# Windowed attention and a snake-activated MLP on one Trainium2 core: where the global rows are turned, cast and placed

## The chip, the core and the metric

The kernel runs on one core of a Trainium2 chip. The metric is the device time of one execution in microseconds (us). The core has five engines with an instruction queue each: TensorE (PE, its weight loads PEld), VectorE (DVE), ScalarE (ACT), GpSimd (POOL) and SyncE (SP). SP computes nothing; it issues DMAs. POOL issues DMAs too, and casts while it loads. Each queue runs in the order in which the program wrote it.

## What is computed

For each of 8 batches there are 8 heads of 576 rows of 64 numbers. A row attends to the rows at most 32 away; 8 rows are global: they see all and are seen by all. The result, 4608 tokens of 512 numbers, goes through two matrix products with a snake activation between them.

```python
def _attn_ref(q, k, v, global_idx):
    scores = scale * np.matmul(q, k.transpose(0, 1, 3, 2))
    mask = np.abs(pos[:, None] - pos[None, :]) <= 32
    mask = mask | is_global[:, None] | is_global[None, :]
    scores = np.where(mask, scores, -1e9)
    attn = softmax(scores)
    return np.matmul(attn, v)

def _moe_ref(x, w_in, w_out, alpha):      # x 4608x512, w_in 512x2048, w_out 2048x512
    h = x @ w_in
    s = np.sin(alpha * h)
    return (h + s * s / (alpha + 1e-09)) @ w_out
```

## The kernel before, in words

The order of all work is written out by hand; waits follow from the tiles that an instruction reads and writes.

**Stages.** After a setup comes attention(0) alone. Then, for b = 0 to 7, gemm1(b) (the product with w_in and the activation), and attention(b+1), with the matmuls of gemm2(b) (the product with w_out) put in between. gemm2(b) is a generator; `fill(n)` issues its next n matmuls (128x512 each) on TensorE. LATE gives these numbers for attention(1) by head pair and third of scores, MIDST those after the last pair, GROUP_LATE those for gemm1(1) by product, 64 in all. What is not used up goes on later.

**Attention of a batch** goes over four head pairs (hp). For each, `scores` makes three groups of four matmuls into a PSUM ring of two (line 737), ScalarE takes the exponential (line 745), VectorE multiplies it by MASK (line 748). The products of the pair before (line 779) stand between: with VX (values) into zn, with OB (ones) into zd. Then `inverse` (lines 805 and 808, ScalarE), `sums` (line 789) and `normalise` (line 811, VectorE) make xT. `beside(hp)` ends a pair: what the caller wants done there. `idle(hp)` issues a 128x512 matmul of ones (`warm`, line 537) whose result nobody reads.

**Tiles of keys, queries and values.** KX, QX and VX exist twice; batch b uses number b % 2. Batch 0's keys and queries are loaded by rows and turned on TensorE (`turn_part`, `place_part`, lines 584 to 605). Batch b > 0: `cast_qk(b)` (POOL, line 328) casts q and k in DRAM to kd and qd, `turn_qk(b)` (SP, line 337) turns them by two DMA transposes into kt and qt, and `place` (VectorE, lines 347 and 354) copies those into KX and QX, in PLACES: four copies of keys, then four of queries. `load_v(b)` (POOL, line 385) loads values, four DMAs for each pair.

**Global rows.** `gather(src, dst)` (SP, line 480) issues eight DMAs that fetch the global rows of all batches: gk, gq and gv. They lie in the rows 13, 14 and 15 of H2 that gemm1 fills later with its products 13 to 15 (gq in 13, gk in 14, gv in 15). `turn_kq` turns gk and gq in eight TensorE transposes (line 701) and casts them on VectorE to kTg and qTg (line 705); `place_globals(b)` (POOL, lines 363 and 368) copies those into KX and QX. `cast_globals_v` (POOL, line 693) casts gv to VGb, from which `load_vg(b)` (SP, line 394) brings eight pieces to VX.

**gemm1(b)** makes 16 products (nt) of eight matmuls (line 967) in three PSUM tiles in turn; each goes through a sine on ScalarE (line 1003), a square on ScalarE if nt is in ON_ACT and otherwise on VectorE (lines 1008 and 1010), and a last step on VectorE (line 1014). In gemm1(0), at nt = 10, POOL has a tiny copy `seen` that waits for kt, and then issues V of batch 1, place_globals(1), w_out (`load_w_out`, line 408) and more V. At nt = 10 to 13 the first two pairs of batch 1's keys and queries are placed; the other two pairs are placed in attention(1), in beside(0) and beside(1).

Before the change the setup queues gk, batch 0's load_vg, gq and gv on SP one after the other; beside(0) of attention(0) places the second half of batch 0, clears VX[1] and QX[1] on POOL, queues cast_globals_v on POOL and the two transposes of batch 1 on SP; beside(1) calls turn_kq; KX[1] is cleared by VectorE in four parts, one in the setup and three in beside(0) to beside(2).

Of the kernel before, what the change touches and what calls it, by code (L numbers as in the profile page):

```python
# [28 lines left out]
PLACES = [(w, t, y) for w in (1, 0) for t in range(2) for y in range(2)]  # L29
# [218 lines left out]
def kernel(  # L248
# [93 lines left out]
    def place(b, which, t, y, copy, hps=slice(0, NHP)):  # L342
# [10 lines left out]
        else:  # L353
# [2 lines left out]
                in_=src.rearrange("p h (i a) -> p h i a", a=24),  # L356
            )

    def place_globals(b):

        for t in range(2):
            rows = slice(t * D, (t + 1) * D)
            nc.gpsimd.tensor_copy(
                out=KX[b % 2][rows, :, :, t * D + KT : t * D + KT + NG],
                in_=kTg[rows, :, None, :, b].to_broadcast([D, NHP, NT12, NG]),
            )
        for y in range(2):
            nc.gpsimd.tensor_copy(
                out=globals_of(b, slice(0, P), y),
                in_=qTg[:, :, None, y::2, b].to_broadcast([P, NHP, 7, 4]),  # L370
            )
# [106 lines left out]
    def gather(src, dst):  # L478
        for j in range(NG):
            nc.sync.dma_start(  # L480
                out=dst[j * B : (j + 1) * B],
                in_=src[:, :, bass.ds(greg[j], 1), :].rearrange("b h o d -> b h (o d)"),
            )
# [73 lines left out]
    load_w_in((2, 3))  # L557
    load_vg(0)
    gather(q, gq)
    gather(v, gv)  # L560


    band = setup.tile([P, 2, 2, WCOL // 2], DT.bfloat16, name="band")
# [69 lines left out]

    gpf = setup.tile([P, 1], DT.float32, name="gpf")
    nc.vector.tensor_copy(out=gpf[:], in_=gp64[:].bitcast(DT.int32)[:, 0:1])
    place_part(1, 0, 0, act)
    nc.scalar.activation(out=qpos[:], in_=qpos[:], func=AF.Square, bias=gpf[:, 0:1], scale=-1.0)
    place_part(1, 0, 1, act)
    gf = setup.tile([P, NG], DT.float32, name="gf")
    nc.vector.tensor_copy(out=gf[:], in_=gidx8[:].bitcast(DT.int32)[:, 0::2])  # L640
    first = setup.tile([P, NG], DT.float32, name="first")
# [12 lines left out]
    )  # L654
    nc.vector.tensor_tensor(out=fone[:], in0=fone[:], in1=cond[:, 2:3], op=ALU.mult)

    nc.vector.memset(KX[1][:, 0], 0.0)
    for n in range(2):
        place_part(0, 0, n, dve)
    for w, name in ((1, "k"), (0, "q")):  # L660
        pg[w] = both[0:D, 32 + w * 64 : 64 + w * 64].bitcast(DT.bfloat16)
        nc.tensor.transpose(
# [29 lines left out]
    def cast_globals_v():  # L692
        nc.gpsimd.tensor_copy(out=VGb[:], in_=gv.rearrange("p h d -> p (h d)"))
# [19 lines left out]
    def attention(b, beside):  # L713
# [101 lines left out]

        start, per_scores = (START, PER_SCORES) if b != 1 else (0, LATE)
        def idle(hp):
            if (b == 0 and hp > 1) or (b == 1 and hp < 3):
                warm(zo[0], 1)

        fill(start)
# [1 line left out]
        for hp in range(NHP):  # L823
            Es[hp] = pairp.tile([P, NT12, WCOL], DT.bfloat16, name="E")
            for g in range(2):
                scores(hp, g)
                fill(per_scores[hp][g])
                idle(hp)
            if b == 0 and hp:
                products(hp - 1, range(3), (1,))  # L830
            elif hp:
                products(hp - 1, (0, 1))
            scores(hp, 2)
            idle(hp)
            if b == 0 and hp:
                products(hp - 1, range(3), (0,))
            elif hp:
                products(hp - 1, (2,))
            if hp:
                inverse(hp - 1)  # L840
                sums(hp - 1, 1)
                sums(hp - 1, 0)
                normalise(hp - 1)
            fill(per_scores[hp][2])
            beside(hp)
# [96 lines left out]


    ON_ACT = (1, 3, 5, 8, 10, 12, 14)
    ON_ACT_FIRST = (1, 3, 4, 6, 7, 9, 10, 11, 12, 13, 14)
    ON_ACT_SECOND = (1, 3, 4, 5, 9, 10, 11, 12, 13, 14)

    def gemm1(b):


        xT = xTs[b]
        r0 = (b % 2) * S
        NE = NG * B // 2
        more = b == B - 1
        W = HALF + (NE if more else 0)
        xg = XG[:].rearrange("p c j b -> p c (j b)")
        hr = tc.alloc_tile_pool(name="hr", bufs=1, space=PSUM)
        hs = {}

        def chunks(nt, cs):  # L960
            if nt not in hs:
                hs[nt] = (zn, None, zd)[nt % 3] or hr.tile([P, 2, 512], DT.float32, name="zr")
            h = hs[nt]
            for c in cs:
                for e in range(2):
                    lhsT = w_in[:, c, nt * P : (nt + 1) * P]
                    nc.tensor.matmul(  # L967
                        out=h[:, e, 0:HALF], lhsT=lhsT, rhs=xT[:, c, e, :],
                        start=(c == 0), stop=(c == CT - 1), skip_group_check=True,
                    )  # L970
                    if more:
                        nc.tensor.matmul(
                            out=h[:, e, HALF:W], lhsT=lhsT, rhs=xg[:, c, e * NE : (e + 1) * NE],
                            start=False, stop=(c == CT - 1), skip_group_check=True,
                        )

        on_act = (ON_ACT_FIRST, ON_ACT_SECOND, ON_ACT)[min(b, 2)]
        for nt in range(NT):
            if b < 2 and 10 <= nt < 14:
                for which, t, y in PLACES[2 * (nt - 10) : 2 * (nt - 9)]:  # L980
                    place(b + 1, which, t, y, nc.vector.tensor_copy, slice(0, NHP if b else 2))
            if b == 1 and nt in (3, 4):
                square_x(0, nt - 3)
            if b == 1 and nt in (6, 8):
                square_w(nt // 2 - 3)
            if b == 0 and nt == 10:

                nc.gpsimd.tensor_copy(out=seen[:], in_=turned[1][1][0:1, 0:1])
                load_v(1, (0,))
                place_globals(1)  # L990
                load_v(1, (1,))
                load_w_out()
                load_v(1, (2, 3))
                load_vg(1)
            if nt == 0:

                for n in range(2):
                    chunks(n, range(CT - 1))
            chunks(nt, range(CT - 1, CT) if nt < 2 else range(CT))
            h = hs[nt]  # L1000
            fill((GROUP_LATE if b == 1 else PER_GROUP)[nt])
            sb = spool.tile([P, 2, HALF + NE], DT.bfloat16, name="sb")
            nc.scalar.activation(  # L1003
                out=sb[:, :, 0:W], in_=h[:, :, 0:W], func=AF.Sin, scale=alphaT[:, nt : nt + 1]
            )
            s2 = spool.tile([P, 2, HALF + NE], DT.bfloat16, name="s2")
            if nt in on_act:
                nc.scalar.activation(out=s2[:, :, 0:W], in_=sb[:, :, 0:W], func=AF.Square)  # L1008
            else:
                nc.vector.tensor_tensor(out=s2[:, :, 0:W], in0=sb[:, :, 0:W], in1=sb[:, :, 0:W], op=ALU.mult)  # L1010
            for dst, lo, hi in (
                (H2[:, nt, r0 : r0 + S], 0, HALF), (HG[:, nt, :], HALF, HALF + NE)
            )[: 1 + more]:
                nc.vector.scalar_tensor_tensor(  # L1014
                    out=dst.rearrange("p (e c) -> p e c", e=2),
                    in0=s2[:, :, lo:hi], scalar=recipT[:, nt : nt + 1], in1=h[:, :, lo:hi],
                    op0=ALU.mult, op1=ALU.add,
                )
        hr.release()
# [50 lines left out]
    START = 2  # L1070
    PER_SCORES = ((1, 11, 3), (3, 3, 4), (3, 3, 4), (3, 4, 5))

    LATE = ((0, 0, 0), (0, 0, 0), (0, 0, 0), (4, 4, 6))
    MIDST = 4
    PER_GROUP = (0, 0, 5) + 11 * (1,) + (0, 0)
    GROUP_LATE = (0, 0, 4) + 10 * (3,) + (4, 4, 4)

    def places_at(b_att, at):
        if b_att == 1 or b_att + 1 == B:
# [5 lines left out]
    def phase_a(b_att, b_moe):  # L1085
        def beside(at):

            if b_moe is None:
                if at == 0:
                    second_half()  # L1090
                    nc.gpsimd.memset(VX[1][:].bitcast(DT.int32), 0)
                    nc.gpsimd.memset(QX[1][:].bitcast(DT.int32), 0)
                    cast_globals_v()
                    turn_qk(1)
                if at == 1:
                    turn_kq()
                if 0 <= at < 3:
                    nc.vector.memset(KX[1][:, at + 1], 0.0)
                return
            if at == 0:  # L1100
                if b_moe == 2:
                    column_norms(zn[:, 0, :])
                if b_moe >= 3:
                    token_norms(b_moe - 3, zn[:, 1, :])
            if 0 <= at < 2 and b_moe:
                square_x(b_moe, at)
            if b_att == 1 and 0 <= at < 2:
                for which, t, y in PLACES[4 * at : 4 * at + 4]:
                    place(1, which, t, y, nc.vector.tensor_copy, slice(2, NHP))
            for which, t, y in places_at(b_att, at):  # L1110
                place(b_att + 1, which, t, y, nc.vector.tensor_copy)
            if b_moe == 0 and at == 2:
                turn_qk(2)
            if b_moe == 1 and at in (2, 3):
                square_w(at)

        if b_moe is not None:
            waiting.append(gemm2(b_moe))
        attention(b_att, beside)
# [67 lines left out]
```

## Time and profile before

| what | value |
|---|---|
| median of 3 runs | 400.41 us (400.18 to 401.48) |
| the profiled execution | 398.71 us, of which the span is 396.9 us |
| granted TensorE clock in it | 0.999 |
| TensorE busy | 343.0 us, 86% of the span |
| ScalarE, VectorE, GpSimd busy | 294.8, 289.5, 129.7 us |
| DMA moved | 38.08 MB, mean 96 GB/s |

A profile is of one execution. Its span runs from the first to the last instruction; the execution's own time also holds what lies around it. A line such as "zo L701 <- DMA H" names the tile that is written, the line of the kernel and, behind the arrow, what ended the wait; buffer numbers are left out, so that gk, gq and gv all appear as H. A wait is put down to one releaser, which need not be the right one where several DMAs write the same tile.

### The profile page before, as it was taken

How to read it: one execution, taken by the hardware profiler on the slowest of the kernel's cores; microseconds unless marked ns; L12 is line 12 of the kernel's file. 1: busy time of each engine (PE TensorE's matmuls, PEld its weight loads, DVE VectorE, ACT ScalarE, POOL GpSimd, SP SyncE). 2: the span in 40 equal slices, each digit the busy share in tenths (PEclk: the TensorE clock that was granted, in tenths of full speed). 3: DMA queues.
4: the chain of work that ended last, by engine and by line, in shares of the span. 5: the costliest groups of instructions: out<-in, count | busy, mean ns of one | idle time of the engine just before them, and what ended most of it. 6: DMA issues, size and time to landing. Idle time of an engine off the chain costs nothing. (4 is left out here: it accounts for less than half of the span.)

```text
span 396.9 us, 8633 instructions
## 1 busy us (share of the span) xinstructions
PE 343.0 (86%) x3175; PEld 233.6 (59%) x3175; DVE 289.5 (73%) x614; ACT 294.8 (74%) x564; POOL 129.7 (33%) x203
## 2 busy tenths in 40 slices
PE   2621888589999889999999999999999999899893
PEld 2511756366666556667666776667667766576341
DVE  6940778857786988897889888888887876588500
ACT  7740699868987978878887888798888888776111
POOL 8890674677204730085008500870000000000001
PEclk9999999999999999999999999999999999999999
DMA  7999899999975794568907991562610001001221
GB/s 119 118 172 158 145 122 175 174 163 136 157 135 87 85 141 90 90 85 95 210 28 86 104 201 55 58 64 43 136 28 28 26 28 55 20 8 28 55 81 46
DMA packets 103579, 38.08 MB, mean 96 GB/s; under 512 B 94138, under 2 KB 98250, under 8 KB 103082
## 3 DMA queue, kind: packets, MB, share of 16 engines
q0 software_dynamic: 56640, 18.56, 40.8%
q1 hardware_dynamic: 46890, 18.89, 22.6%
q8 instruction: 27, 0.44, 0.5%
q14 instruction: 22, 0.18, 0.2%
HBM read 37.15 MB, written 17.83 MB: 139 GB/s over the span
## 5 line engine op out<-in xcount | busy, mean ns | idle before, releaser
L1027 PE MATMUL zo<-w_out,H 128*128 128x512 bf16 x576 | 152.7, 378 | 0.0
L967 PEld LDWEIGHTS <-w_in 128*128 128x128 bf16 x1024 | 99.3, 97 | 47.4 <-issue 16.1
L385 POOL DMA_DIRECT2D VX<-in_v_dram x128 | 83.7, 667 | 121.1 <-PE zd L779 103.3
L745 ACT ACTIVATE E<-ring 128x480 bf16<-128x480 f32 x96 | 54.3, 569 | 41.9 <-PE ring L737 41.3
L1027 PEld LDWEIGHTS <-H 128*128 128x128 bf16 x576 | 52.1, 97 | 38.0
L967 PE MATMUL zn<-xT,w_in 128*128 128x288 bf16 x384 | 57.3, 285 | 4.1 <-DVE H L1014 3.8
L748 DVE TENSOR_TENSOR E<-E,MASK 128x480 bf16<-128x480 bf16 x96 | 38.2, 428 | 17.7 <-ACT E L745 16.3
L967 PE MATMUL zr<-xT,w_in 128*128 128x288 bf16 x320 | 47.9, 285 | 1.2 <-DVE H L1014 0.7
L967 PE MATMUL zd<-xT,w_in 128*128 128x288 bf16 x320 | 46.6, 285 | 0.9 <-DVE H L1014 0.7
L1014 DVE SCALAR_TENSOR_TENSOR H<-s,recipT,zn 128x576 bf16<-128x576 bf16 x48 | 39.0, 813 | 9.2 <-ACT s L1008 5.9
L737 PE MATMUL ring<-QX,KX 128*128 128x120 bf16 x384 | 37.7, 223 | 9.3 <-ACT E L745 4.3
L1008 ACT ACTIVATE s<-sb 128x576 bf16<-128x576 bf16 (+1 forms) x63 | 43.4, 689 | 2.0
L1003 ACT ACTIVATE sb<-zn,alphaT 128x576 bf16<-128x576 f32 (+1 forms) x48 | 35.6, 741 | 12.2 <-PE zn L967 8.8
L737 PEld LDWEIGHTS <-KX 128*128 128x128 bf16 x384 | 28.4, 101 | 24.2 <-issue 9.7
L1055 POOL DMA_INDIRECT out_dram<-osb,grow x1 | 1.0, 1004 | 125.6 <-SPq L1155 125.6
L1014 DVE SCALAR_TENSOR_TENSOR H<-s,recipT,zd 128x576 bf16<-128x576 bf16 x40 | 32.6, 814 | 7.3 <-ACT s L1008 5.3
L1010 DVE TENSOR_TENSOR s<-sb 128x576 bf16<-128x576 bf16 (+1 forms) x65 | 30.1, 464 | 8.4 <-ACT sb L1003 8.2
L1014 DVE SCALAR_TENSOR_TENSOR H<-s,recipT,zr 128x576 bf16<-128x576 bf16 x40 | 32.5, 813 | 5.1 <-ACT s L1008 3.0
L1033 ACT COPY osb<-zo 128x512 f32<-128x512 f32 x36 | 20.8, 578 | 20.4 <-PE zo L1027 20.4
L1003 ACT ACTIVATE sb<-zd,alphaT 128x576 bf16<-128x576 f32 (+1 forms) x40 | 29.7, 741 | 6.9 <-PE zd L967 3.8
L779 PEld LDWEIGHTS <-VX 128*128 128x128 bf16 x448 | 26.5, 100 | 12.2 <-issue 6.8
L1003 ACT ACTIVATE sb<-zr,alphaT 128x576 bf16<-128x576 f32 (+1 forms) x40 | 29.6, 739 | 4.4 <-PE zr L967 3.3
(158 smaller groups left out, 448.5 us busy)
## 6 DMA issues: line engine op xcount, KB each, us to landing
VX<-in_v_dram POOLq DMA_DIRECT2D x128, 36.0 KB, 2.7
kd<-in_k_dram POOLq DMA_DIRECT2D x7, 576.0 KB, 6.1
qd<-in_q_dram POOLq DMA_DIRECT2D x7, 576.0 KB, 9.0
w_in<-in_moe_w_in_dram POOLq DMA_DIRECT2D x4, 512.0 KB, 8.9
w_out<-in_moe_w_out_dram POOLq DMA_DIRECT2D x4, 512.0 KB, 10.0
out_dram<-osb SPq DMA_DIRECT2D x8, 256.0 KB
out_dram<-osb SPq DMA_DIRECT2D x8, 224.0 KB
out_dram<-osb SPq DMA_DIRECT2D x8, 192.0 KB
```

What stands on the lines that cost most here:

```text
L385: nc.gpsimd.dma_start(out=VX[b % 2][r : r + 24, hp, :, t * D : t * D + D], in_=v[b, 2 * hp + t].rearrange("(i a y) d -> y a i d", a=24, y= ...
L737: nc.tensor.matmul(out=ps[:, e * WCOL : (e + 1) * WCOL], lhsT=kx[:, hp, i, :], rhs=qx[:, hp, :, s0 : s0 + 60], start=True, stop=True, skip ...
L745: nc.scalar.activation(out=Eg, in_=ps[:, 0 : 4 * WCOL], func=AF.Exp, scale=scale, accum_out=EA[:, n : n + 1])
L748: nc.vector.tensor_tensor(out=Eg, in0=Eg, in1=MASK[:, 4 * g : 4 * g + 4, :].rearrange("p i c -> p (i c)"), op=ALU.mult,)
L779: nc.tensor.matmul(out=out_t[:, half, :, a - half * CUT : z - half * CUT], lhsT=OB[:] if key else VXb[:, hp, i, :], rhs=E[:, i, :, a - s0 ...
L967: nc.tensor.matmul(out=h[:, e, 0:HALF], lhsT=lhsT, rhs=xT[:, c, e, :], start=(c == 0), stop=(c == CT - 1), skip_group_check=True,)
L1003: nc.scalar.activation(out=sb[:, :, 0:W], in_=h[:, :, 0:W], func=AF.Sin, scale=alphaT[:, nt : nt + 1])
L1008: nc.scalar.activation(out=s2[:, :, 0:W], in_=sb[:, :, 0:W], func=AF.Square)
L1010: nc.vector.tensor_tensor(out=s2[:, :, 0:W], in0=sb[:, :, 0:W], in1=sb[:, :, 0:W], op=ALU.mult)
L1014: nc.vector.scalar_tensor_tensor(out=dst.rearrange("p (e c) -> p e c", e=2), in0=s2[:, :, lo:hi], scalar=recipT[:, nt : nt + 1], in1=h[:, ...
L1027: nc.tensor.matmul(out=ops[:], lhsT=H2[:, nt, blk * P : (blk + 1) * P], rhs=w_out[:, nt, :], start=(nt == 0), stop=(nt == NT - 1),)
L1033: nc.scalar.copy(out=osb[:], in_=ops[:])
```

## The change

- v's global rows are gathered behind the two transposes of batch 1 in SP's queue, in beside(0), and no longer in the setup.
- turn_kq moves from beside(1) of attention(0) into gemm1(0), ahead of product 9. cast_globals_v moves from beside(0) into gemm1(0), at nt = 10, behind the first four V loads and ahead of place_globals(1).
- In the setup the placing of the first half of batch 0's queries (VectorE) comes ahead of the small mask operations, and both halves of the keys (ScalarE) ahead of a square. KX[1] is cleared in four parts in beside(0) to beside(3).
- In attention(1) the keys of the last two pairs are still placed in beside(0); their queries are placed in pair 1 ahead of inverse, sums and normalise of pair 0, and no longer in beside(1).
- The matmuls of ones in pair 2 of attention(1) go; eight matmuls of gemm2(0) take their place (LATE), taken from gemm1(1) (GROUP_LATE).
- In gemm1(0) the squares of products 4 and 6 go to VectorE, that of 5 to ScalarE.

```diff
+    def place_rest(which):
+        for w, t, y in PLACES:
+            if w == which:
+                place(1, w, t, y, nc.vector.tensor_copy, slice(2, NHP))
...
     gather(q, gq)
-    gather(v, gv)
...
-    place_part(1, 0, 0, act)
+    for n in range(2):
+        place_part(1, 0, n, act)
     nc.scalar.activation(out=qpos[:], in_=qpos[:], func=AF.Square, bias=gpf[:, 0:1], scale=-1.0)
-    place_part(1, 0, 1, act)
+    for n in range(2):
+        place_part(0, 0, n, dve)
...
-    nc.vector.memset(KX[1][:, 0], 0.0)
-    for n in range(2):
-        place_part(0, 0, n, dve)
...
-            if (b == 0 and hp > 1) or (b == 1 and hp < 3):
+            if (b == 0 and hp > 1) or (b == 1 and hp < 2):
                 warm(zo[0], 1)
...
+            if b == 1 and hp == 1:
+                place_rest(0)
             if hp:
                 inverse(hp - 1)
...
-    ON_ACT_FIRST = (1, 3, 4, 6, 7, 9, 10, 11, 12, 13, 14)
+    ON_ACT_FIRST = (1, 3, 5, 7, 9, 10, 11, 12, 13, 14)
...
+            if b == 0 and nt == 9:
+                turn_kq()
             if b == 0 and nt == 10:
                 nc.gpsimd.tensor_copy(out=seen[:], in_=turned[1][1][0:1, 0:1])
                 load_v(1, (0,))
+                cast_globals_v()
                 place_globals(1)
...
-    LATE = ((0, 0, 0), (0, 0, 0), (0, 0, 0), (4, 4, 6))
+    LATE = ((0, 0, 0), (0, 0, 0), (2, 3, 3), (4, 4, 6))
-    GROUP_LATE = (0, 0, 4) + 10 * (3,) + (4, 4, 4)
+    GROUP_LATE = (0, 0, 4) + 5 * (2, 3) + (3, 3, 3)
...
                     nc.gpsimd.memset(QX[1][:].bitcast(DT.int32), 0)
-                    cast_globals_v()
                     turn_qk(1)
-                if at == 1:
-                    turn_kq()
-                if 0 <= at < 3:
-                    nc.vector.memset(KX[1][:, at + 1], 0.0)
+                    gather(v, gv)
+                if 0 <= at < NHP:
+                    nc.vector.memset(KX[1][:, at], 0.0)
...
-            if b_att == 1 and 0 <= at < 2:
-                for which, t, y in PLACES[4 * at : 4 * at + 4]:
-                    place(1, which, t, y, nc.vector.tensor_copy, slice(2, NHP))
+            if b_att == 1 and at == 0:
+                place_rest(1)
```

## The prediction

> **What bounds the kernel now.** I read the page first (engine shares, slices), then TensorE's waits by stretch, then the table by stage, then the timeline around the largest waits.
>
> ```profile
> PE 343.0 (86%) x3175; PEld 233.6 (59%) x3175; DVE 289.5 (73%) x614; ACT 294.8 (74%) x564; POOL 129.7 (33%) x203
> PE   2621888589999889999999999999999999899893
> ```
> TensorE is at 9 tenths in nearly every slice after the eighth; its waits after 92 us sum to less than 10 us, so time won before 92 us is kept to the end unless a transfer is late. The low slices are the second to fourth and the eighth. TensorE's waits over 0 to 49 us and over 70 to 92 us name their causes:
>
> ```profile
> PE zo L701 <- DMA H<-in_v_dram: 13.8, 1, 13.8
> PE ring L737 <- DVE QX L347: 3.6, 1, 3.6
> ```
> The timeline shows the first as a stop of all three compute engines (columns: start, duration, engine, line, operation, in brackets the idle time before it):
>
> ```profile
> 23.43 0.69 PE L701 MATMUL zo<-idf,H 64*128 64x64 f32 x4
> 37.95 0.66 PE L701 MATMUL zo<-idf,H 64*128 64x64 f32 x4 [13.84 <-DMA H<-in_v_dram]
> 39.16 0.57 ACT L745 ACTIVATE E<-ring 128x480 bf16<-128x480 f32 x1 [14.68 <-PE ring L737]
> ...
> 21.49 7.31 SPq L480 DMA_DIRECT2D H<-in_q_dram  x8
> 28.98 9.42 SPq L480 DMA_DIRECT2D H<-in_v_dram  x8
> 38.69 2.38 SPq L337 DMA_TRANSPOSE kt<-kd  x1
> 41.18 2.03 SPq L337 DMA_TRANSPOSE qt<-qd  x1
> ```
> turn_kq turned the four blocks of gk at 23.43; the four of gq waited. The waits' view names v's gather, but the semaphore records put the last landing of gq at 37.71, just ahead of 37.95, so gq itself was late. From 33.2 to 37.7 its DMAs landed 0.9 us apart, while GpSimd's queue moved kd, qd and two quarters of w_in (landed 30.0, 32.8, 36.1, 39.5); after that burst v's last six landed within 1.5 us.
>
> **Part 1, the wait for gq.** turn_kq leaves attention(0). The scores of its third pair then stand right behind line 779's matmuls, and the exponential at 39.16 can start when ScalarE is free, 14.68 us earlier: **-14.7**. What could be late next: V of pairs 2 and 3 landed at 27.4 at the latest, and w_in's last quarter (39.48) is first read at product 12, near 50 then. In gemm1(0), product 9 stands about 10 us after the stage's start, near 45, with gq there since 37.7: 7 us of cover, each us beyond it costs one.
>
> **Part 2, GpSimd's copies.** place_globals(1) now stands behind turn_kq's new place, so attention(0) loses this:
>
> ```profile
> 45.58 2.91 DVE L748 TENSOR_TENSOR E<-E,MASK 128x480 bf16<-128x480 bf16 x3
> 46.38 1.84 POOL L363 COPY KX<-kTg 64x384 bf16<-64x384 bf16 x2
> 48.28 0.76 POOL L368 COPY QX<-qTg 128x112 bf16<-128x112 bf16 x2
> 51.54 3.04 POOL L408 DMA_DIRECT2D w_out<-in_moe_w_out_dram  x4
> ```
> Three mask products took 2.91 against 1.21 for three in attention(1); TensorE waited 0.89 and 0.58 for them: **-1.4**. In gemm1(0) the copies meet VectorE's placing copies (eight of 0.31) and squares; bounds 0 and their whole 2.6, I take **+0.5**, since most squares there are ScalarE's and the large product reads PSUM. GpSimd's memsets of VX[1] and QX[1] (26.5 to 30.4) now lie beside attention(0)'s mask products; no row shows such an overlap, the nearest (the copies) would give 1.7, I take 0. The Trainium skill (SBUF — State Buffer, "Who interferes with whom") has a two-input VectorE instruction block only against a GpSimd instruction that reads SBUF, and VectorE copies in a two-port mode against any. By it the memsets cost those products nothing, and the placing copies could wait the whole 2.6 in gemm1(0); the sum would be 2.1 worse.
>
> **Part 3, TensorE's clock of work.** After the 13.84 us of idleness 14 matmuls of line 779 took 1.36 at 40.17 and 42.15, but 0.79 from 44.57 on; ScalarE idled 0.17 and 1.31 beside them. Without the idleness TensorE has worked since 21.8. Bounds 0 and -1.5: **-1.0**.
>
> **Part 4, the setup.** VectorE's QX copies (3.67 us from 11.51) move ahead of seven small operations and lose a 0.70 memset in front of them; the first scores waited 0.86 for them. The mask work then comes behind, so not all is won: between 0 and -0.9, **-0.5**. The memset returns in attention(0) after a normalisation, under TensorE's products.
>
> **Part 5, gemm1(0).** ScalarE had 19.74 busy of 21.1 us there, VectorE 16.86. ScalarE gives one square away (0.68); VectorE gets it (0.46) and turn_kq's two casts (0.42 + 0.41); TensorE gets 1.35 of transposes on 17.6. The new sums, 19.1, 18.1 and 18.9, are all under the old 19.74, but closer together: -0.7 to +0.9, **0**.
>
> **Part 6, the queries of batch 1.**
>
> ```profile
> 75.87 1.21 DVE L748 TENSOR_TENSOR E<-E,MASK 128x480 bf16<-128x480 bf16 x3
> 78.16 0.76 DVE L811 TENSOR_TENSOR xT<-zn,R 128x576 bf16<-128x576 f32 x1 [0.45 <-ACT R L808]
> 78.84 1.26 DVE L347 COPY QX<-qt 64x576 bf16<-64x576 bf16 x4
> 80.16 0.38 PE L737 MATMUL ring<-QX,KX 128*128 128x120 bf16 x4 [3.61 <-DVE QX L347]
> ```
> The copies start at 77.08, where the mask products end, and end near 78.34 instead of 80.10: **-1.75**. The sums and the normalisation behind them end some 0.6 later; they release the next pair's products, which came 0.9 after the scores (81.02) and now stand behind five filling matmuls as well, so that is hidden.
>
> **Part 7, the fillings.** Eight matmuls of gemm2(0) (four took 1.02 to 1.03, some 0.21 each in a row) leave gemm1(1), where TensorE was busy 27.87 of 28.8 us: -1.7. They stand in attention(1) in place of three idle ones: +1.05. Net **-0.65**.
>
> **Part 8, the transfers that come behind.** SP now issues kt when kd has landed (30.0), qt at 32.8, then v's gathers. One hardware queue serves them behind gq, so kt lands some 3 us after 37.7, near 41, qt near 44 (from issue to landing they took 4.4 and 5.6 before). Each SP DMA waits for the landing of the one eight before it: v's seventh for kt, its eighth for qt, so gv is complete near 46 (41.3 before). load_vg(1) is queued behind on SP, and on GpSimd everything behind the cast. turn_kq's casts at product 9 come near 47, so place_globals(1) runs 47.5 to 50.3, four V issues take 2.6, and w_out is issued near 53.2, **1.7 later** than 51.54. Its quarters and V of pairs 2 and 3 had landed at 58.2, 60.8, 64.6, 66.6, 67.8, 69.1; they become 59.9 to 70.8. attention(1) starts near 53.5 (70.5 less the 17.1 of parts 1 to 5), its third pair's fillings near 62 find two quarters, the fourth pair's near 65 and 67 want those of 66.3 and 68.3, its products want V of 69.5. That is a wait of about **+2.0** in all; bounds 0 (kt, qt and gv as quick as without the burst) and +6 (turns and gv 4 us later).
>
> **Sum:** -14.7 - 1.4 + 0.5 - 1.0 - 0.5 + 0 - 1.75 - 0.65 + 2.0 = **-17.5**. The profiled execution took 398.71 (span 396.9 and 1.8 around it), giving 381.2; the median of the runs, 400.41, stands 1.70 above it: 382.9. Since five terms are small overlaps that need not all add, I say **383.5**.
>
> **Rivals.** (1) The transfers become the bound. For: kt and qt of batch 2 took 6.3 and 9.8 us from issue to landing while GpSimd's queue was full, and the new place of batch 1's is inside such a burst. With these, kt lands at 44.0, qt at 53.8, gv at 56.1, w_out is issued at 61.9 (10.4 late), V of pair 3 lands at 79.5. Its products stood at 89.53, so 10.0 is won there, and 1.7 in gemm1(1): 400.4 - 11.7 = **388.7**. Against: the burst ends at 39.5, and GpSimd issues nothing big until kt has landed. Chance 0.11.
> (2) Slower: v's rows hold GpSimd's queue so long that w_out and V of batch 1 come later than before in spite of the earlier start. V of pair 3 would have to land after 91.2 (89.53 + 1.7), 22.1 late, so gv after 67.8; at 70 the time would be **402.6**. For: cast, place_globals, V and w_out are all in one queue behind that landing. Against: kt and qt at 9.8 each and eight gathers at 0.92 end at 64.7. Chance 0.03.
> (3) The change doesn't remove the wait, it moves: product 9 waits for gq, or the placing at product 10 for kt. gq would have to be 7 us later than it was; then half of part 1 is left, **391**. Chance 0.03; nothing in the queue ahead of gq changes.
>
> **Numbers.** The forecast 0.83, the rivals 0.11, 0.03 and 0.03. Low end: every term at its better bound is -21.6, but V of pair 3 cannot land before 69.1 + 1.7, which allows 18.7 at that point and 1.7 after: 400.4 - 20.4 = **380**. High end: part 2 at +1.2, parts 3 and 4 at 0, part 5 at +0.9, part 6 at -1.0, part 7 as it is and part 8 at +6 leave -8.3: **392**, which holds rivals 1 and 3; the memsets' 1.7 on top of all these is left out. A difference under 0.3% (1.2 us) cannot be told from none. Faster 0.95 (the forecast, rivals 1 and 3, less a little of rival 1's tail), same 0.01, slower 0.04.
>
> **What would show it.** Right: no TensorE wait over 3 us between 20 and 35; the first sine near 34 to 35 instead of 51.8; line 701 inside gemm1(0), with no wait over 0.5; the wait on line 347 near 1.9; gemm1(1) starting near 74 to 75 with w_out issued near 53. Wrong: a wait of several us for w_out or VX in attention(1) (rival 1), GpSimd's cast after 67 (rival 2), line 701 waiting in gemm1(0) (rival 3), or attention(0) lasting as long as before because its mask products run beside the memsets.

## The result, and the profile after

The changed kernel takes **387.28 us** (median of 4 runs, 385.56 to 388.72), the kernel before 400.95 beside it (4 runs, 400.18 to 403.95). The ratio is 0.9644, 95% interval 0.9579 to 0.9708: 13.7 us faster in the medians. The profiled execution took 387.46, its span is 385.7 against 396.9. Executions that took over 1.5% longer than the fastest of their kernel are left out of the ratios here.

The two rows of the page that answer to those of before (TensorE's busy time, then its busy tenths in 40 slices):

```profile
PE 340.7 (88%) x3124; PEld 233.6 (61%) x3172; DVE 289.7 (75%) x615; ACT 294.2 (76%) x563; POOL 130.2 (34%) x203
PE   2578966899998899899998999999999999899893
```
The third and fourth slices, 2 and 1 before, are 7 and 8 now. Two slices of 6 are left, the sixth and seventh, from 48 to 68 us: the end of gemm1(0) and attention(1). TensorE's two largest waits there, over 50 to 82 us (us in total, times, longest):

```profile
PE zo L1035 <- DMA w_out<-in_moe_w_out_dram: 2.9, 2, 1.7
PE ring L740 <- DVE QX L347: 2.0, 1, 2.0
```
Between 16 and 50 us no wait for a DMA is left. What was cut out by stage, from each profile (attention(0) begins with its first exponential, gemm1(b) with its first sine; f1 and g1 are experiments below):

| stage, us | before | after | e1 | f1 | g1 |
|---|---|---|---|---|---|
| setup | 15.97 | 16.75 | 15.99 | 16.09 | 16.72 |
| attention(0) | 35.82 | 18.94 | 18.50 | 17.86 | 18.72 |
| gemm1(0) | 20.66 | 21.48 | 22.28 | 22.09 | 21.75 |
| attention(1) | 19.77 | 23.57 | 22.15 | 19.68 | 19.49 |
| gemm1(1) | 26.84 | 26.41 | 27.79 | 27.83 | 26.87 |
| the rest | 277.84 | 278.55 | 278.2 | 278.1 | 277.6 |

16.9 us are won in attention(0), and 3.8 of them are lost again in attention(1). The loss starts in SP's queue (timeline after, columns: start, duration, engine, line, operation):

```profile
21.56 7.31 SPq L485 DMA_DIRECT2D H<-in_q_dram  x8
29.91 9.91 SPq L337 DMA_TRANSPOSE kt<-kd  x1
39.92 2.72 SPq L337 DMA_TRANSPOSE qt<-qd  x1
42.83 6.97 SPq L485 DMA_DIRECT2D H<-in_v_dram  x8
```
SP began to issue kt's transpose at 29.91, as kd landed, and was held in that one issue for 9.91 us, where it took 2.38 before. v's eight gathers stood behind it and went out 0.86 apart. GpSimd's queue (and VectorE's placing copies between) shows what followed:

```profile
51.38 0.60 POOL L696 CAST VGb<-H 64x512 bf16<-64x512 f32 x1 [5.50 <-DMA H<-in_v_dram]
51.71 1.33 DVE L347 COPY QX<-qt 64x576 bf16<-64x576 bf16 x2
51.94 1.83 POOL L368 COPY KX<-kTg 64x384 bf16<-64x384 bf16 x2
53.83 0.78 POOL L373 COPY QX<-qTg 128x112 bf16<-128x112 bf16 x2
53.92 0.86 DVE L347 COPY QX<-qt 64x576 bf16<-64x576 bf16 x2
57.12 3.04 POOL L413 DMA_DIRECT2D w_out<-in_moe_w_out_dram  x4
```
The cast waited 5.50 us for gv, and w_out was issued at 57.12 instead of 51.54. TensorE's timeline in attention(1), and its granted clock a little later (from, to, busy us and counts of PE, PEld, DVE, ACT and POOL, granted clock, DMA share, GB/s):

```profile
63.30 0.39 PE L740 MATMUL ring<-QX,KX 128*128 128x120 bf16 x4 [2.03 <-DVE QX L347]
65.98 0.59 PE L1035 MATMUL zo<-w_out,H 128*128 128x512 bf16 x1 [1.23 <-DMA w_out<-in_moe_w_out_dram]
66.36 0.58 PE L782 MATMUL zn<-E,VX 128*128 128x88 bf16 x4
72.79 1.02 PE L1035 MATMUL zo<-w_out,H 128*128 128x512 bf16 x4 [1.66 <-DMA w_out<-in_moe_w_out_dram]
```
```profile
66.00:69.00 3.00, 3.00 (x33) 2.73 (x33) 0.00 (x0) 0.45 (x1) 0.72 (x2) 0.50 1.34 210
```
There are two waits for w_out, 2.89 together, and behind the stops of 2.03 and 1.23 a stretch at half the clock, from 65.6 to 69.0 us, in which four matmuls take 0.58 instead of 0.36. The seven groups from 66.36 to 69.04 take 2.68; in f1 the same seven, with an idle matmul of 0.22 among them, take 1.68 (63.07 to 64.75).

### The profile page after: what moved, and what is told of

Its sections match the earlier page's. It is cut to its first block, busy times and chain, and to the rows that moved or that the text cites. A ratio compares the mean times of both kernels' runs of the same rounds, so it can differ in the third digit from the quotient of the medians.

```text
span 385.7 us, 8582 instructions
## 1 busy us (share of the span) xinstructions
PE 340.7 (88%) x3124; PEld 233.6 (61%) x3172; DVE 289.7 (75%) x615; ACT 294.2 (76%) x563; POOL 130.2 (34%) x203
## 5 line engine op out<-in xcount | busy, mean ns | idle before, releaser
L1035 PE MATMUL zo<-w_out,H 128*128 128x512 bf16 x528 | 142.9, 379 | 4.9 <-DMA w_out<-in_moe_w_out_dram 2.9
L751 DVE TENSOR_TENSOR E<-E,MASK 128x480 bf16<-128x480 bf16 x96 | 36.1, 409 | 20.0 <-ACT E L748 18.5
L1018 DVE TENSOR_TENSOR s<-sb 128x576 bf16<-128x576 bf16 (+1 forms) x66 | 31.4, 476 | 7.0 <-ACT sb L1011 6.7
L782 PEld LDWEIGHTS <-VX 128*128 128x128 bf16 x448 | 26.6, 100 | 13.7 <-issue 8.6
L1011 ACT ACTIVATE sb<-zr,alphaT 128x576 bf16<-128x576 f32 (+1 forms) x40 | 29.6, 740 | 5.1 <-PE zr L972 3.8
```

What stands on the lines that cost most here:

```text
L751: nc.vector.tensor_tensor(out=Eg, in0=Eg, in1=MASK[:, 4 * g : 4 * g + 4, :].rearrange("p i c -> p (i c)"), op=ALU.mult,)
L782: nc.tensor.matmul(out=out_t[:, half, :, a - half * CUT : z - half * CUT], lhsT=OB[:] if key else VXb[:, hp, i, :], rhs=E[:, i, :, a - s0 ...
L1011: nc.scalar.activation(out=sb[:, :, 0:W], in_=h[:, :, 0:W], func=AF.Sin, scale=alphaT[:, nt : nt + 1])
L1035: nc.tensor.matmul(out=ops[:], lhsT=H2[:, nt, blk * P : (blk + 1) * P], rhs=w_out[:, nt, :], start=(nt == 0), stop=(nt == NT - 1),)
```

## The experiments

The theory after the result: turn_kq's new place alone makes the gain, and what is given back in attention(1) comes from transfers (gv, then w_out and V in GpSimd's queue) and from TensorE's clock after a stop. The rivals: the setup, the fillings, or the shares of DMA.

| kernel | ratio to before, 95% | span, us |
|---|---|---|
| the change | 0.9644 (0.9579 to 0.9708) | 385.7 |
| e1 turn_kq alone | 0.9627 (0.9605 to 0.965) | 384.9 |
| e2 v's rows ahead again | 0.9567 (0.9541 to 0.9592) | 385.5 |
| e3 w_out first | 0.9613 (0.9585 to 0.9641) | 384.6 |
| e4 old setup order | one execution | 386.6 |
| f1 turn_kq and the queries | 0.9591 (0.9547 to 0.9635) | 381.7 |
| f2 old fillings | 0.9766 (0.9723 to 0.981) | 391.6 |
| f3 f1, VG pieces late | no interval | 385.2 |
| f4 e1 with a warm stop | 0.9594 (0.9554 to 0.9634) | 382.7 |
| g1 f1 and new fillings | 0.9532 (0.9503 to 0.9561) | 381.1 |
| g2 f1, V of pair 2 first | 0.9552 (0.9521 to 0.9583) | 383.3 |
| g3 both | 0.9583 (0.9555 to 0.9611) | 383.0 |

**e1: the kernel before, with turn_kq alone moved.**

```diff
-                if at == 1:
-                    turn_kq()
...
+            if b == 0 and nt == 9:
+                turn_kq()
```


> The kernel before with one edit: turn_kq moved to product 9 of gemm1(0). Theory (the 13.84 us were gq's lateness alone, and v's place in SP's queue has no part in that gain): the third pair's exponential of attention(0) comes near 24.5 instead of 39.16, the first sine near 35 instead of 51.8. SP's queue is as before (kt issued near 38.7 in 2.4 us), the cast of v's rows stands near 41.5, so w_out is issued near 53 to 54, and TensorE waits under 1 us for it. Span 381 to 384, so no longer than the changed kernel's 385.7. Rival (the parts need each other: with v's gathers still ahead of the transposes, product 10 or pair 2 of attention(1) waits for kt, qt or V): a wait of several us in gemm1(0) on line 354 or 347, span over 388.

One moved call gives as much as the whole change. w_out went out at 52.85 and nothing waited for it. The span, 384.9, is above the 381 to 384 that was hoped for, and the stage table says where: attention(1) took 22.15 against 19.77, with the same wait in it as before (TensorE's timeline, and the granted clock behind the stop):

```profile
64.47 0.58 PE L737 MATMUL ring<-QX,KX 128*128 128x120 bf16 x4 [3.60 <-DVE QX L347]
```
```profile
64.40:70.90 6.50, 6.43 (x51) 4.83 (x52) 1.59 (x6) 3.39 (x9) 3.86 (x7) 0.53 1.48 154
```
The kernel before had the same stop (3.61 us, ending at 80.16), and kept its clock; its row for the stretch with the stop in it:

```profile
76.40:84.00 7.60, 3.99 (x60) 3.02 (x57) 4.41 (x14) 4.59 (x13) 7.40 (x12) 1.00 1.78 181
```

**e2: the change, with v's gather ahead of the transposes on SP.**

```diff
-                    turn_qk(1)
                     gather(v, gv)
+                    turn_qk(1)
```


> The changed kernel with v's gathers ahead of the two transposes in beside(0). Theory (w_out came 5.6 us late because SP was held 9.9 us by the first transpose's issue, v's gathers came one by one behind, and GpSimd's queue held w_out behind the cast): the first transpose is issued after 38 in about 2.4 us, the cast stands near 41.5 to 43.5, place_globals near 48, w_out is issued near 53.5 instead of 57.1. TensorE's waits for w_out fall from 2.9 us to under 1, the first sine of gemm1(1) comes 3 to 4 us earlier (near 77), span near 382. Rival (attention(1) became longer because of the eight matmuls added to its third pair, or the transfer's own speed): span within 1 us of 385.7.

In the profile the expectation missed. gv was there early, but now kt was late: it landed at 45.70, and GpSimd, idle for 16 us, waited for it with `seen`. w_out went out at 54.92, 2.2 earlier than in the change, and TensorE's wait for it stayed (over 50 to 85 us):

```profile
PE zo L1035 <- DMA w_out<-in_moe_w_out_dram: 3.5, 2, 2.8
```
In this profile and the change's the queue on SP in front of GpSimd's work is the cost, in whichever order the two stand. But the profiled execution took 387.19. Of the four others two took 383.09 and 383.42, with spans of 381.4 and 381.7, near the 382 that was expected, and two 389.66 and 391.81. No profile shows those, so what this order is worth stays open.

**e3: the change, with w_out ahead of the cast on GpSimd.**

```diff
                 load_v(1, (0,))
+                load_v(1, (1,))
+                load_w_out()
                 cast_globals_v()
                 place_globals(1)
-                load_v(1, (1,))
-                load_w_out()
```


> The changed kernel with w_out and pair 1's V ahead of the cast and of place_globals(1) in GpSimd's queue; SP's queue is untouched. Theory (what counts is when w_out is issued): w_out is issued near 48.5 instead of 57.1, no wait of TensorE for it, place_globals(1) ends near 55 to 56, just ahead of the first scores of attention(1), which may wait up to 1 us for it. The first sine of gemm1(1) near 76.5 to 78, span 381 to 383. Rival (SP's and the hardware queue's lateness itself binds: load_vg(1) behind the late gather): attention(1) stays 3 us longer, span 385 to 387.

w_out went out at 48.26 and nothing waited for it. gv landed at 55.74, GpSimd's copies stood behind it until 58.8, and TensorE waited for them at the start of attention(1):

```profile
PE ring L740 <- POOL QX L373: 5.1, 1, 5.1
PE ring L740 <- DVE QX L347: 2.0, 1, 2.0
```
The wait only changed its name; around it the clock was at half, from 57.0 to 63.9 us. The first sine of gemm1(1) came at 79.90 against 80.74.

**e4: the change, with the setup's order of before** (keys, square, keys; queries behind the mask work; KX's first clearing still in beside(0)).

> The changed kernel with the setup's order of before (placing of the first half of the queries behind the small mask operations, the square between the two halves of the keys; the memset stays out of the setup). Theory (the new order made ScalarE's first key copies wait for the second group of transposes, 10.25 instead of 8.30): the first exponential comes at 15.2 to 16.0 instead of 16.75, the first sine of gemm1(0) near 34.9. Since attention(1) is bound by when w_out lands, which hangs on SP and not on the setup, little of it is left at the first sine of gemm1(1): under 0.4 us there. Rival (the stages only follow one another): 0.8 us earlier to the end, first sine of gemm1(1) near 79.9, span near 384.9.

The first exponential came 1.78 earlier than in the change (14.97), the first sine of gemm1(0) 1.81 earlier, and the first sine of gemm1(1) 0.33 later (81.07). What the setup won didn't reach the end of attention(1), as the theory had it. That transfers alone took it back isn't shown: in this one execution the clock was at half twice there, from 56.3 to 59.7 and from 66.5 to 69.9 us, and once in the change.

**f1: e1, and the queries of batch 1 placed ahead of inverse and normalise** (the two calls of place_rest, as in the change).

> The kernel before with two edits: turn_kq at product 9 of gemm1(0), and the last queries of batch 1 placed ahead of inverse, sums and normalise. Theory (attention(1) of the run with turn_kq alone lasted 22.2 us instead of 19.8 because TensorE's clock fell to 0.53 after the 3.6 us stop on line 347): the stop becomes 1.8 to 2.0 us, the clock stays at 1.0 from 60 to 80, attention(1) lasts 17.5 to 18.5 us, the first sine of gemm1(1) comes near 75, span 380.5 to 382. Rival (the transfers of w_out and V set the end of attention(1)): a new wait for w_out or V of 1 to 3 us, first sine of gemm1(1) at 77 or later, span 383 or more.

383.66 us in the median (383.39 to 386.17). The wait for line 347 fell from 3.60 to 1.76, the clock stayed at 1.00 (62 to 68 us), and attention(1) went from 22.15 to 19.68. It fell short of the hoped-for 17.5 to 18.5, because the next thing was late and took 1.7 back:

```profile
PE zn L784 <- DMA VX<-in_v_dram: 1.7, 1, 1.7
```
V of pairs 2 and 3 stands behind w_out in GpSimd's queue; its pieces landed from 67.06 to 69.38.

**f2: the change, with LATE, GROUP_LATE and the idle matmuls of before.**

> The changed kernel with LATE, GROUP_LATE and the matmuls of ones as before (no gemm2(0) in the third pair of attention(1)). Theory (the eight matmuls added there wait for w_out, which came 5.6 us late, so they cost what they should have won, and by their stop a stretch at half clock): the stop at 65 to 66 goes, no half clock in attention(1), waits for w_out under 2 us and only in the fourth pair, first sine of gemm1(1) 1.5 to 3 us earlier (78 to 79), span 383 to 384.5. Rival (the fillings win 0.65 us as forecast and w_out's landing sets the end anyway): first sine within 0.7 of 80.7, span 385.5 to 386.5.

The theory fell here. The old fillings made the kernel slower by 4.9 us (medians 392.15 and 387.28), where part 7 gave 0.65 for them:

```profile
PE zn L782 <- DMA VX<-in_v_dram: 6.5, 1, 6.5
PE ring L740 <- POOL QX L373: 2.3, 1, 2.3
```
In the change w_out reaches TensorE as a wait in front of fillings; without those fillings TensorE runs on to the products and waits for V instead, until 75.14. The eight fillings are work done in a time that is waited out anyway. But more than half of the 4.9 is the clock. From the products behind the last wait of the stage to the first sine, f2 takes 9.74 us at a mean clock of 0.69, the change 6.79 at 1.00 (f2, then the change):

```profile
75.14:84.88 9.74, 9.69 (x86) 7.20 (x88) 3.19 (x9) 5.46 (x11) 6.41 (x11) 0.69 1.27 173
73.95:80.74 6.79, 6.74 (x85) 5.24 (x87) 3.29 (x9) 5.25 (x11) 5.32 (x9) 1.00 1.06 179
```
That is 3.0 us. In f2 the clock was at half from 70.9 to 81.2 us; it fell in a stop of 6.46 us that no filling broke up. The products themselves began 1.19 later (75.14 and 73.95), about as much as w_out was issued later in this profile (58.29 and 57.12). The mean clock of f2's four executions was 0.977 to 0.987, that of the change's four 0.990 to 0.999.

**f3: f1, with the VG pieces of batch 2 issued later** (`load_vg(2)` behind `turn_qk(2)`), to see whether those small SP transfers take w_out's share.

> As the kernel with turn_kq and the queries moved, and load_vg(2), eight small pieces on SP's queue, issued behind the transposes of batch 2 instead of ahead of attention(1). Theory (w_out's first quarter takes 5 to 6 us from issue since those pieces share the 16 engines): the first quarter lands 1 to 2.5 us sooner after its issue; if transfers set the end of attention(1), the first sine of gemm1(1) is up to 2 us earlier. Rival (they are too small to matter): landing and first sine within 0.5 us of the run without this edit.

The rival held for the landing: w_out was issued at 53.34 and its first quarter landed 5.87 us later, against 6.30 in f1. The first sine of gemm1(1) came at 76.63 against 75.72, and gemm1(1) and attention(2) grew to 53.3 us against 49.5. The moved pieces stand in SP's queue ahead of batch 3's transposes: the first of these went out at 102.66 instead of 96.80 and held SP for 11.64 us, VectorE waited 2.48 for its kt, and TensorE 3.57 for VectorE. The four executions took from 386.91 to 400.80.

**f4: e1, with 14 matmuls of ones put into the stop.**

```diff
             fill(per_scores[hp][2])
+            if b == 1 and hp == 1:
+                warm(zo[0], 14)
             beside(hp)
```


> The kernel before with turn_kq at product 9 of gemm1(0), and 14 matmuls of ones more at the end of the second pair of attention(1), where TensorE waits 3.6 us for line 347 in any case (3.0 us of work at full clock, read by nobody). Theory of the clock: the stop at 60.8 to 64.4 is filled, the clock stays at 1.0 (0.53 without them), the matmuls behind take 0.37 instead of 0.60 for four, attention(1) lasts 19.5 to 20 us instead of 22.2, span 382 to 383. Rival (the slow stretch has another cause, or the wait is what counts): attention(1) stays at 22 us, span within 0.7 of 384.9.

They hide no work and shorten nothing that is waited for; they only keep TensorE busy until the queries are there. The time fell (median 384.74 against 385.93), attention(1) from 22.15 to 19.77. The matmuls behind the stop, and the clock:

```profile
64.13 0.38 PE L737 MATMUL ring<-QX,KX 128*128 128x120 bf16 x4 [0.58 <-DVE QX L347]
```
```profile
60.00:70.00 10.00, 9.08 (x98) 5.76 (x98) 6.28 (x18) 6.52 (x18) 4.38 (x8) 1.00 1.44 178
```
From the end of the stop to the first sine it is 12.06 us here and 14.45 in e1, which puts the clock's part in e1's profile at 2.4 us. The medians differ by 1.2, and the intervals overlap; the mean clock was 0.997 in three of f4's four executions and 0.985 to 0.992 in e1's four. With 2.4 f1 adds up too: 1.84 less of wait, 2.4 less by the clock, 1.7 more for V make 2.5, and 2.47 was measured.

**g1: f1 with the new fillings.** Its diff is LATE's third row, GROUP_LATE and hp < 2, as in the change.

> f1 with the filling matmuls of the changed kernel (eight of gemm2(0) in pair 2 of attention(1) in place of three idle ones, eight fewer in gemm1(1)). Theory (what the old-fillings run taught): they stand in a stretch in which TensorE waits 1.7 us for V of pair 2 anyway, so attention(1) does not get longer (first sine of gemm1(1) at 75.7, within 0.3) and gemm1(1) gives up to 1.7 back: span 380.5 to 381.5, against 381.7. Rival: V's landing is not what they hide behind, they add their 1.05 to attention(1) and gemm1(1), which is paced by ScalarE, gives back no more than the 0.4 of the changed kernel: span 382.0 to 382.5.

382.50 us (6 runs, 381.55 to 382.81), faster than both kernels: its interval lies under that of the change. As the theory had it, attention(1) didn't grow (19.49 against 19.68) with eight matmuls more in it, and gemm1(1) gave back 0.96. The wait for V took up the difference:

```profile
PE ring L742 <- DVE QX L347: 1.8, 1, 1.8
PE zn L784 <- DMA VX<-in_v_dram: 0.9, 1, 0.9
```

**g2: f1 with V of pair 2 ahead of w_out.**

```diff
-                load_v(1, (1,))
+                load_v(1, (1, 2))
                 load_w_out()
-                load_v(1, (2, 3))
+                load_v(1, (3,))
```


> f1 with V of pair 2 of batch 1 issued ahead of w_out on GpSimd (2.6 us of issue earlier in the queue for it, 2.6 later for w_out). Theory: V of pairs 2 and 3 behind w_out ends attention(1); V of pair 2 then lands near 56 instead of 68.6, the wait of 1.7 for it goes, the quarters of w_out land near 60, 63, 66 and 69 and are read from 65, 66, 68.5 and 70 on: first sine of gemm1(1) 74.0 to 74.6 against 75.7, span 380.0 to 380.8. Rival: w_out is the bound and the wait only changes its name: a wait for w_out of over 1 us, first sine 75.5 to 76, span 381.5 to 382.

Neither came. No wait for V or w_out was left, yet attention(1) took 19.57. The half clock had come at the start of the stage, behind a stop of 1.22 us:

```profile
57.87 0.49 PE L742 MATMUL ring<-QX,KX 128*128 128x120 bf16 x4 [1.22 <-ACT E L750]
58.15 0.63 PE L542 MATMUL zo<-ones 128*128 128x512 bf16 x1
```
```profile
58.00:60.00 2.00, 2.00 (x15) 1.41 (x14) 1.56 (x5) 1.69 (x6) 2.00 (x4) 0.50 1.17 172
```
The profiled run was the slowest of six (385.02; the others 381.62 to 383.54), so what the order is worth with the clock up stays open; the medians, 383.40 and 382.50 for g1, don't speak for it.

**g3: g1 and g2 together.**

> Both of the former: V of pair 2 ahead of w_out and the filling matmuls of the changed kernel. Theory: with V there the eight fillings are no longer hidden and cost their 1.05 in attention(1) (first sine 75.0 to 75.6), and need quarters of w_out from 62 on, which land near 60 and 63 (a wait up to 0.7); what is left over in gemm1(1) is won back only in part: span 380.3 to 381.5, no better than V first alone. Rival: gemm1(1) gives 1.7 back: span 379.3 to 380.0.

The fillings now come before their quarters of w_out, which stands 2.6 later in the queue (TensorE's waits over 50 to 90 us):

```profile
PE zo L1036 <- DMA w_out<-in_moe_w_out_dram: 2.2, 1, 2.2
```
The median is 384.32 us, above that of either half. In f1, g1 and g3 TensorE waits 0.9 to 2.2 us for whichever of V and w_out stands second in GpSimd's queue. In g2 it waited for neither, in a stage that had run at half clock from 58.0 to 61.4 us, which may have hidden a wait.

## Why the prediction was right, and where it was not

Direction and mechanism were right, and 387.28 lies inside the range; the number itself was 3.8 too low. By steps, with the two profiles' spans, where 17.5 were forecast and 11.2 came (by the medians of both kernels it is 13.7):

**Right.** Part 1: the third pair's first exponential came at 25.18 instead of 39.16, 13.98 earlier, or 14.76 without the 0.78 by which the setup was later; forecast 14.7. No idle time stands before it, and gq was there for its transposes:

```profile
25.18 0.55 ACT L748 ACTIVATE E<-ring 128x480 bf16<-128x480 f32 x1
44.78 0.70 PE L704 MATMUL zo<-idf,H 64*128 64x64 f32 x8
```
The eight transposes run in one go, with no wait in front. Parts 2 and 3: from that exponential to the first sine it took 10.51 instead of 12.63, 2.1 less; forecast 2.4 in attention(0). No run separates the two. Of part 3, the slow pace did not go with the idleness, it became shorter: 14 products still took 1.35 at 25.73 and 0.96 at 27.70, and 0.79 from 29.35 on, where before the pace was slow from 38.6 to 44.1. (The clock column says 1.00 there all the same: the record of the clock begins at 28.05 us in the change and at 44.15 in the kernel before.) The mask products of the last pair took 0.98, as against 2.91 beside GpSimd's copies. Those beside GpSimd's memsets (25.76 to 29.6) were not held up: two in 0.66.

```profile
31.13 0.98 DVE L751 TENSOR_TENSOR E<-E,MASK 128x480 bf16<-128x480 bf16 x3
```
Part 6: the wait for line 347 went from 3.61 to 2.03, 1.58 against 1.75. In gemm1(0), parts 2 and 5, +0.83 against +0.5: the placing copies, 0.62 for two elsewhere, took 1.33 and 0.86 beside GpSimd's copies (the rows at 51.71 and 53.92 above). The Trainium skill (SBUF — State Buffer, "Who interferes with whom") has VectorE's copies in a two-port mode and any GpSimd instruction block each other, and a VectorE instruction with two SBUF inputs contend only with a GpSimd instruction that reads SBUF. The trace agrees with both halves: about 1.0 us lost by the copies, nothing by the mask products beside the memsets.

**Wrong: part 8, and the step in it was "kt near 41, qt near 44, gv complete near 46".** kt and qt came close (42.62, 44.66). gv was complete at 51.32. The sum let SP issue v's gathers while the transposes were in flight; in fact kt's issue itself held SP until 39.82, a time at which GpSimd's burst was still on its way. The gathers then began at 42.83, not behind the two transposes' issue near 35. So w_out was 5.6 late, not 1.7, and waits of 2.9 stood where 2.0 was forecast. That is halfway to the first rival (w_out at 61.9, gv at 56.1; 388.7 us), to whose time the result is nearer. The rival's cause, kt 6.3 us and qt 9.8 us from issue to landing, came in another form: kt took 12.71 and qt 4.74.

**Wrong: a term that wasn't there.** After the stops of attention(1) TensorE ran at half its clock from 65.6 to 69.0 us, which cost at least 1.2 (2.68 against 1.68 less 0.22 for the same seven groups). Part 3 reckoned with the clock in attention(0) alone. attention(1) then adds up: fillings +1.05, w_out +2.9, clock +1.2, queries -1.6 make +3.55 of the +3.80 in the table; the sum of the prediction had +1.3 there.

**Wrong in size: part 7, and a term beside it.** gemm1(1) gave back 0.43, not 1.7. The fillings alone gave more: 0.96 from f1 to g1, 1.11 from f2 to the change, 2.10 from g2 to g3. But gemm1(1) had grown without them: it took 27.52 to 28.00 us in the six other kernels with the old fillings (e1, f1 to f4, g2) and 26.84 before, and the sum had nothing for that. GpSimd was busy 7.0 us of that stage before and 19 to 22 in e1, f1, f2 and g2, with loads and copies, and VectorE's squares took 0.62 on average in f1 instead of 0.45; whether that is the whole cause is open. In attention(1) the fillings' cost was hidden behind late transfers, as g1 shows against f1, where the kernel as a whole gains 1.2 (383.66 and 382.50, with intervals that overlap).

**Part 4, the setup: not settled by the one profile.** It showed +0.78 where -0.5 was forecast, but ScalarE began its key copies in it only when the second group of transposes was done. Four profiles of thirteen show that: the change, and with the old order g1, g2 and g3. The first key copy in the change, and in e2 with the same order:

```profile
10.25 3.23 ACT L604 COPY KX<-zn 64x288 bf16<-64x288 bf16 x8 [3.44 <-PE zd L588]
```
```profile
8.41 3.23 ACT L604 COPY KX<-zn 64x288 bf16<-64x288 bf16 x8 [1.60 <-PE zn L588]
```
Like with like: with the early start the new setup's first exponential comes at 15.18, 15.24 and 15.47 (e2, f2, e3), the old one's at 15.97 to 16.36 (before, e1, f1, f3, f4), so -0.8; with the late start at 16.75 (the change) and at 16.65 to 16.72 (g1, g2, g3), no gain. e4, with the old order and the early start but without the memset, came at 14.97, which speaks for the memset rather than for the order as the source. Why an execution starts late is open; g1 to g3, all late, ran on one chip, e1 to e4 and f1 to f4, all early, on two others. None of it reached the end: e4 lost its 1.8 before gemm1(1).

These add up: setup 1.3, attention(0) and gemm1(0) 0.6, attention(1) 2.5 and gemm1(1) 1.3 over the sum, and 0.7 in the stages behind, which one execution can differ by (those stages take 277.6 to 279.2 us in all profiles but f3's).

## What to carry to other kernels

Move the piece of work that waits, not its neighbours: one call moved behind its data gave the whole gain, and the rest of the change bought some of it and sold some. When an issue is moved to an earlier place in a queue, ask until when that one issue can hold the queue, not only when its data lands, and follow what stands behind it to the engine that waits. A stop costs more than its length when the clock drops behind it, and several short ones close together can do that too, so idle time ahead of a transfer that will be late anyway is worth filling with real work.

## What the runs showed of the hardware

An issue is not short because its queue is free: the same DMA transpose held SP 2.38 us, or 9.91 us when it was issued into GpSimd's burst of transfers. In all four profiles in which it stands ahead of v's gathers (the change, e3, e4, f2) it took 8.96 to 9.97 us, in the nine others 2.11 to 2.54. In the change it ended at 39.82, near the end of that burst (last landing 40.92). That the burst is the reason is argued and was not tried by itself; gq's gathers, on SP's own queue, landed until 38.23 too.

The granted clock after a stop isn't a function of the stop's length. A stop of 3.6 us left it at 1.00 in the kernel before and at 0.53 for 6.5 us in e1; stops of 2.03 and 1.23, which ended 2.7 us apart, went with 0.50 in the change, and one of 1.22 in g2. What decides in these traces is how the stops lie in a grid of 3.41 us. In every profile the clock changes at whole multiples of 3.41 us behind its first change, and it stays at half for 3.41 us (the change), 6.83 (e1) or 10.24 (f2). Two neighbouring stretches of that grid in e1, two in the change, two in the kernel before (columns as in the rows of the clock above: behind the length TensorE's busy time, and the clock third from the end):

```profile
60.26:63.67 3.41, 0.61 (x9) 0.40 (x7) 2.59 (x8) 2.12 (x5) 1.30 (x2) 1.00 1.28 204
63.67:67.08 3.41, 2.61 (x21) 2.06 (x22) 1.53 (x5) 1.32 (x4) 0.65 (x1) 0.50 1.45 188
62.18:65.59 3.41, 1.41 (x11) 0.82 (x13) 2.95 (x9) 1.98 (x6) 1.28 (x2) 1.00 1.24 185
65.59:69.01 3.42, 3.03 (x33) 2.74 (x33) 0.00 (x0) 0.46 (x1) 0.73 (x2) 0.50 1.34 211
74.87:78.28 3.41, 1.68 (x33) 1.40 (x30) 2.54 (x10) 2.61 (x7) 1.92 (x4) 1.00 1.70 150
78.28:81.69 3.41, 1.53 (x25) 1.30 (x26) 2.19 (x6) 1.11 (x4) 3.41 (x6) 1.00 2.09 173
```
e1's stop lies almost whole in one stretch, and the next one is slow; the same stop in the kernel before is cut by the border at 78.28, and 1.68 and 1.53 us of work stand beside its two parts. In the thirteen traces a stretch in which TensorE was busy for 1.41 us or less was followed by one at half clock every time (14 cases), one at full clock with 1.63 us or more never; of six between, two were. That equal kernels can keep their clock or lose it fits this, since the grid lies elsewhere in each trace: the profiled execution of the kernel before had 0.999 and took 398.71, the 25 others whose clock is on record had 0.983 to 0.995 and took 399.13 to 402.60.

The Trainium skill (TensorE: Matmul & The Clock Gate, "Part 1: The HAM clock gate") has the clock halved after at least one idle window of about 3.4 us, in windows that run freely. A free window explains why equal stops end differently, and its length is that of the grid; that a window must be idle as a whole is not what the change and g2 show, in which TensorE worked for 1.41 and 1.62 us of it between shorter stops.
